# Four-layer attention backward on one core: chunk 0 of the window layers in 16 visits, layer 1's first visits inside the last linear tile

## The chip, the cores and the metric

The kernel runs on one core of a Trainium2 chip. The metric is the device time of one execution in microseconds (us): the median of repeated runs. A profile is one further execution, recorded instruction by instruction; its times are counted from the first instruction. Engines are named as in the profile: PE (TensorE; PEld are its weight loads), DVE (VectorE), ACT (ScalarE), POOL (GpSimd), SP (the queue that issues nearly every DMA).

## What is computed

A stack of four residual layers over x of shape [2048, 640] in bfloat16, and its gradient for a given `grad_out`: the output, the gradient of x, and those of four weight matrices.

```python
x = x + A(layernorm(x))   # layer 0: linear attention
x = x + B(layernorm(x))   # layer 1: sliding window
x = x + A(layernorm(x))   # layer 2
x = x + B(layernorm(x))   # layer 3
out, vjp = jax.vjp(f, x, wqkv_A, wo_A, wqkv_B, wo_B); grads = vjp(grad_out)
```

`A` has 32 heads of 20 columns with feature map `phi` and no softmax. `B` has the same heads, a causal softmax over a window of 256 rows.

## The kernel before, in words

Rows are handled in 16 tiles of 128 (`TT`), two tiles to a chunk (8 chunks). The stages follow each other: the forward of all layers (`forward`); the backward of layer 3's window attention (`core`); the linear backward of layer 2 (`plan_linear`, 16 tiles); `core` again for layer 1; then layer 0's linear backward together with the weight gradients.

**The order is written out by hand.** Each stage makes a list of (due slot, function), sorts it, and runs it slot by slot (`slots`, `plan`); the due slots are the lists in `PLACES`. Every engine executes its own instructions strictly in the order so recorded, SP's DMAs among them, so an instruction that waits holds all that stand behind it on its engine.

**A core** walks over visits (`core_visits`, `core_visit`). A visit has up to four blocks of 128 queries by 128 keys for two heads. In it PE makes the scores `s` (one PSUM buffer, pool `pS`), ACT makes `e = exp(s)`, POOL masks diagonal and far blocks (L803, L807). Three visits later PE makes `dp` (one PSUM buffer, `pD`) and DVE makes `ds = dp * e` (L792). Four visits later PE transposes `ds` (L814), and `st.lag` = 6 visits later it multiplies `ds` and `e` into `acc`. So the next `s` waits for the last `e`, and the next `dp` for the last `ds`. Chunk 0 has no earlier keys: six blocks where other chunks have twelve, in 24 visits of two blocks; chunks 1 to 7 have 24 visits each of up to four. In chunk 0 each visit also issues 8 transposes of the identity whose result is not used (`warm`, `thin` in `core`).

**Each chunk needs its gradients first** (`plan_before`): load `gb` and `ob` by DMA, transpose `gb` (`flip`), multiply by `WoT` (`prod`, L913 on DVE), sum over each head (`fold`, `split`: L921, L923, L930, L932, on POOL but for one tile of layer 1's chunk 0, which is on DVE) and transpose `ds` into `dT` (`flip8`, L941, copied by ACT at L942). For chunk c+1 this is spread over chunk c's visits; for chunk 0 it stands at the end of the stage before. The keys and queries of a quarter chunk come as slabs (`core_loads`), fetched one quarter ahead on SP.

**At the start of layer 3's core** the last slots of the forward (`tail`, up to seven) run as hooks of the first visits. The weights `WTB` (2.46 MB) come in one DMA at visit 15.

**At the start of layer 1's core** the last linear tile ends first: its products `dh` (PE, taken out of PSUM by ACT at L1184), `ln` (DVE L1193, L1195; the sum with the handed-over gradient on POOL at L1196), `ln2` (ACT L1203, POOL L1204) and the store `g<-lgn`. Then `core` begins. The slabs take over the memory of the linear stage's loads. The linear stage rotates over six PSUM buffers.

Of the kernel before, what the change touches and what calls it, by code (L numbers as in the profile page):

```python
# [15 lines left out]
P = 128  # L16
# [55 lines left out]
    sd=[0.7, 0, 0, 3, 3, 3, 3, 3.9, 0, 0, 3.2, 2.6, 3.3, 3.1],  # L72
    dj=[3, 21.9, 24, 3.5, 0.7, 8])


class Kern:
# [121 lines left out]

    def fetch(self, w, src):
        self.dma(w.rearrange("p a b -> p (a b)"), src)  # L200

# [82 lines left out]
    def forward(self, st):  # L284
# [108 lines left out]
        def begin_slabs():  # L393
            early.close()
            self.core_slabs(3, st.core)
            self.core_buffers(st, st.core)
        plan += [(END - 32, begin_core), (END - 6, begin_slabs)]
# [4 lines left out]
        def before(a):  # L402
            if a == 0:
                first_.update(enumerate(self.slots(self.plan_before(st, 3, 0, st.core, ((1, 2, 3, 4.5, 10), (2, 4, 5, 10, 12))), 16)))
            if first_[a] is not None:
                first_[a]()
# [301 lines left out]
    def core_visits(self, st, l, S, c, qr, dq):  # L708

        t0 = 2 * c  # L710
        w0 = max(t0 - 2, 0)
        for p in range(2):
            if c == 0:
                order = [[(0, 0), (1, 0), (1, 1)]] * 2
            else:
                order = [[(0, 0), (0, 1), (1, 1), (0, 2), (1, 2), (1, 3)], [(0, 0), (0, 1), (0, 2), (1, 2), (1, 3), (1, 1)]]
            units = [(gi, bi, kk) for gi in range(2) for bi, kk in order[gi]]
            m = len(units) // 3
            for v in range(3):
# [11 lines left out]
                u.first, u.last = v == 0, v == 2  # L731
                u.n = 24 * c + 6 * qr + 3 * p + v
                u.by_dma = self.by_dma(u.n)
                yield u
# [7 lines left out]
    def order(n):  # L742

        return ("FPA", "PFA", "PAF", "FAP", "AFP", "APF")[PLACES["fo"][n % 24] if 48 <= n < 192 else 0]

    WARM = (8, 5)
    TAIL = 5
# [11 lines left out]
    def core_visit(self, st, l, u, piece, on_act, thin):  # L759
# [63 lines left out]
        self.tick(0.5)  # L823
        for k in self.order(len(h) - 1):
            if parts[k] is not None:
                parts[k]()
# [61 lines left out]

    def plan_before(self, st, l, c, B, at=None, l0=0, quick=False):

# [10 lines left out]
        for i, (f0, p0, p1, sp, f8) in enumerate(at):  # L901
# [14 lines left out]
            def fold(i=i, t=t):  # L916
                R = B.ring[t % 4]
                assert x["n", i] == 2
                pr = x["pr", i] = B.sf.tile([P, H, DH], F32, name="prod")
                eng = nc.vector if quick and i == 0 else nc.gpsimd  # L920
                eng.tensor_tensor(out=pr, in0=R["ds"][:, :, 0:DH], in1=self.heads(x["o"][:, i, :]), op=ALU.mult)  # L921
# [3 lines left out]
            def split(i=i, t=t):  # L925
                R = B.ring[t % 4]
                m = DH // 4
                ds, pr = R["ds"], x["pr", i][:, :, 0:m]
                eng = nc.vector if quick and i == 0 else nc.gpsimd
                eng.tensor_scalar(out=ds[:, :, DH:DH + m], in0=pr, scalar1=-1.0, scalar2=None, op0=ALU.mult)  # L930
# [163 lines left out]
    def plan_linear(self, st, lp, l, t, X, WT, g_out):  # L1094

        nc = self.nc
        sv = self.sv[l]
        i = t % 2
# [88 lines left out]
        def ln():  # L1187
# [7 lines left out]
            nc.vector.tensor_scalar(out=x["s1"], in0=ac[:, 0:1], scalar1=ac[:, 1:2], scalar2=-1.0 / D, op0=ALU.add, op1=ALU.mult)  # L1195
            nc.gpsimd.tensor_tensor(out=x["dh"], in0=x["dh"], in1=L["g"][:, i, :], op=ALU.add)  # L1196

        def ln2():
            L = X[t // 2]
            if i == 0:  # L1200
                L["gn"] = lp.lo.tile([P, 2, D], BF, name="lgn")
            assert "s1" in x
            nc.scalar.activation(x["a"], L["hn"][:, i, :], ACT.Identity, bias=x["s1"], scale=x["s2"])  # L1203
            nc.gpsimd.tensor_tensor(out=L["gn"][:, i, :], in0=x["dh"], in1=x["a"], op=ALU.add)  # L1204
            if i == 1:
                self.put(13, self.pair(g_out, t // 2), L["gn"])
# [122 lines left out]

    def core_slabs(self, l, B):  # L1330
# [4 lines left out]
    def core_buffers(self, st, B):  # L1335
        st.lag = 6
        st.pe = self.pool(B.es, "pe", st.lag + 1, side=B.side)
        st.pd = self.pool(B.es, "pd", st.lag - 2, side=B.side)
        st.pt = self.pool(B.es, "pt", st.lag - 2, side=B.side)
# [42 lines left out]
    def core(self, st, l, g_out, B, hooks):  # L1382

        NC = TT // 2

        plan = []
        dq = {}
        for c in range(1, NC):
            plan += [(32 * (c - 1) + a, *f) for a, *f in self.plan_before(st, l, c, B)]
        for c in range(NC):  # L1390
# [6 lines left out]
        rest = [(max(a - off, 0), f) for a, f, *_ in plan if a * 0.75 >= nv]  # L1397
        rest = self.slots(rest, int(max(a for a, _ in rest)) + 1)

# [5 lines left out]
        on_act = [PLACES["xx"][n % 24] for n in range(nv)]  # L1405
        n = 0
        with ExitStack() as es:
            st.pS = self.pool(es, "pS", 1, bass.MemoryType.PSUM, "right")
            st.pD = self.pool(es, "pD", 1, bass.MemoryType.PSUM, "right")
            st.hist = []  # L1410
            for c in range(NC):
                for qr in range(4):
                    S = B.slabs.pop(0)
                    for i, u in enumerate(self.core_visits(st, l, S, c, qr, dq)):
                        for k, f in enumerate(hooks):
                            if int(k * 0.75) == n:
                                f()
# [4 lines left out]
                        if n == st.lag:  # L1422
                            st.pA = self.psum(es, "pA", 1)
                            dqp = self.pool(B.dqs, "dqp", 3, side="right")
                        if n % 24 == st.lag:
                            dq[c] = dqp.tile([P, 2, QT], BF, name="dq")
                        self.core_visit(st, l, u, slots[n], on_act[n], thin[n])
                        n += 1
            for _ in range(st.lag):
                self.core_visit(st, l, None, slots[n], on_act[n], thin[n])  # L1430
                n += 1
        return rest

# [12 lines left out]
    def passes(self):  # L1446
# [6 lines left out]
        with ExitStack() as rest:  # L1453
# [5 lines left out]
            def switch():  # L1459
                keep.close()  # L1460
                self.rest_pools(st, es)
            assert n3 <= 7
            hooks = tail[:-1] + [lambda: (tail[-1](), switch())] + [lambda: None] * (7 - n3)

            hooks += [lambda: None] * (70 - len(hooks))
            hooks[20] = lambda: self.fetch(st.WTB, self.WT["B"])
            hooks[40] = lambda: self.fetch(st.WoTA, self.WoT["A"])
            left3 = self.core(st, 3, self.gs[2], st.core, hooks)
            for f in left3[:8]:
# [7 lines left out]

            psl, le, lw, w1 = ExitStack(), ExitStack(), ExitStack(), ExitStack()
            WTA = self.pool(lw, "wa", 1).tile([P, NF, D], BF, name="WTA")
            st.ps = self.psum(psl, "pl", 6)  # L1480
            lp, B = self.linear_pools(lw, "left", 0), S()
# [14 lines left out]
            for t in range(TT):  # L1496
                plan += [(max(base + 8 * t + a, 0), f) for a, f in self.plan_linear(st, lp, 2, t, X, WTA, self.gs[1])]

            def begin():
                self.flush()  # L1500
                le.close()
                self.core_slabs(1, B)
            b0 = base + 8 * (TT - 1) + PLACES["n1"][0]
            plan.append((b0, begin))
            fs = self.plan_before(st, 1, 0, B, (PLACES["n1"][1:6], PLACES["n1"][6:11]), -10, True)
            plan += [(b0 + a, f) for a, f, *_ in fs if a < 20]
            hooks = self.slots([(a - 20, f) for a, f, *_ in fs if a >= 20], 8)
            for f in self.slots(plan, int(max(a for a, _ in plan)) + 1):
# [4 lines left out]
            lw.close()  # L1513
            psl.close()
            st.ps = st.ps2
            yield

            self.core_buffers(st, B)
            left1 = self.core(st, 1, self.gs[0], B, [f or (lambda: None) for f in hooks])
            for f in left1[:8]:  # L1520
# [136 lines left out]
```

## Time and profile before

| | |
|---|---|
| three runs | 2153.57, 2156.81 (median), 2165.6 us |
| the profiled execution, first to last instruction | 2161.7 us |
| PE busy | 2022.5 us (94%) |
| DVE, ACT, POOL busy | 1396.7, 1313.6, 1034.4 us |
| the forward of all layers | 0 to 665 us |
| layer 3's core, visits of chunk 0 | 665 to 708 us |
| layer 2's linear stage, full pace | 1138 to 1228 us |
| the last linear tile and layer 1's chunk 0 | 1228 to 1281 us |

The profiled execution is 4.9 us longer than the median of the runs. The view of stretches of the span gives, for each stretch, the time that each engine was busy and "PEclk", the clock that TensorE was granted as a share of full speed; it takes only the values 1 and 0.5, so an average between them tells what part of the stretch ran at half speed. The view in order of time gives, for a group of equal instructions, start, duration, engine, line, operation, what is written and read, and in brackets how long the engine had been idle before it and what ended that.

### The profile page before, as it was taken

How to read it: one execution, taken by the hardware profiler on the slowest of the kernel's cores; microseconds unless marked ns; L12 is line 12 of the kernel's file. 1: busy time of each engine (PE TensorE's matmuls, PEld its weight loads, DVE VectorE, ACT ScalarE, POOL GpSimd, SP SyncE). 2: the span in 40 equal slices, each digit the busy share in tenths (PEclk: the TensorE clock that was granted, in tenths of full speed). 3: DMA queues.
4: the chain of work that ended last, by engine and by line, in shares of the span. 5: the costliest groups of instructions: out<-in, count | busy, mean ns of one | idle time of the engine just before them, and what ended most of it. 6: DMA issues, size and time to landing. Idle time of an engine off the chain costs nothing.

```text
span 2161.7 us, 77035 instructions
## 1 busy us (share of the span) xinstructions
PE 2022.5 (94%) x32885; PEld 1566.0 (72%) x32885; DVE 1396.7 (65%) x2828; ACT 1313.6 (61%) x1866; POOL 1034.4 (48%) x1643
## 2 busy tenths in 40 slices
PE   8989998899988999999989999999998989999999
PEld 6667776677766877777768778777776888888644
DVE  7788886788854888888748769888886233320000
ACT  6558887478875787777637667777775133330000
POOL 1046666156666577777524466777765211220000
PEclk9999999999998999999989989999999999999999
DMA  7597876699984379988889824899888899989650
GB/s 253 195 230 205 215 203 174 199 228 213 221 204 135 94 160 189 189 191 180 185 269 265 213 82 102 191 191 191 177 181 204 272 296 250 267 203 276 194 164 21
DMA packets 658937, 425.46 MB, mean 197 GB/s; under 512 B 399264, under 2 KB 629408, under 8 KB 658208
## 3 DMA queue, kind: packets, MB, share of 16 engines
q1 hardware_dynamic: 658592, 420.52, 76.7%
q8 instruction: 257, 4.21, 0.8%
q14 instruction: 88, 0.72, 0.1%
HBM read 195.17 MB, written 144.70 MB: 157 GB/s over the span
## 4 chain that ended last, share of the span: by engine, by line
PE 51%; DVE 8%; DMA 7%; ACT 6%; issue 4%; POOL 3%; SPq 2%; DVEq 0%; ACTq 0%; POOLq 0%
PE dense L187 17%; PE wg L187 14%; DVE ds L792 5%; PE acc L187 4%; PE dp L187 3%; PE flip L207 3%; PE flip L814 2%; DMA pqb<-pqk 2%; SPq L131 2%; ACT e L788 2%; PE flip L218 1%; PE sT L187 1%; PE ops L187 1%; ACT eT L450 1%; ACT dsT L819 1%
## 5 line engine op out<-in xcount | busy, mean ns | idle before, releaser
L792 DVE TENSOR_TENSOR ds<-dp,e 128x1024 bf16<-128x1024 f32 (+1 forms) x384 | 444.0, 1156 | 122.0 <-PE s L187 76.7
L788 ACT ACTIVATE e<-s 128x1024 bf16<-128x1024 f32 (+1 forms) x384 | 375.0, 976 | 113.5 <-PE s L187 94.9
L450 ACT ACTIVATE eT<-sT 128x2048 bf16<-128x2048 f32 x180 | 338.3, 1880 | 94.9 <-PE sT L187 77.9
L187 PE MATMUL wg<-rhs,lhs 128*128 128x240 bf16 (+3 forms) x2880 | 372.2, 286 | 4.4 <-DMA lhs<-o 4.4
L187 PEld LDWEIGHTS <-lhs 128*128 128x128 bf16 x2880 | 261.4, 98 | 92.3 <-DMA lhs<-o 5.4
L807 POOL TENSOR_SCALAR_AFFINE_SELECT e<-e 128x256 bf16<-128x256 bf16 x512 | 207.5, 420 | 166.7 <-ACT e L788 163.4
L187 PEld LDWEIGHTS <-dqT 128*128 128x128 bf16 x1920 | 174.0, 98 | 61.5 <-issue 4.4
L458 POOL TENSOR_SCALAR_AFFINE_SELECT eT<-eT 128x512 bf16<-128x512 bf16 x256 | 163.8, 644 | 107.1 <-ACT eT L450 103.2
L187 PE MATMUL acc<-slabqs,ds 128*128 128x20 bf16 x2880 | 195.9, 172 | 2.6 <-ACT dq L876 0.3
L187 PE MATMUL acc<-ds,e 128*128 128x20 bf16 x2880 | 193.6, 171 | 0.0
L187 PEld LDWEIGHTS <-ds 128*128 128x128 bf16 x2880 | 173.3, 96 | 19.7 <-issue 15.3
L187 PE MATMUL dp<-slabT,dT 32*128 32x128 bf16 (+1 forms) x1952 | 150.0, 244 | 28.5 <-DVE ds L792 22.6
L803 POOL TENSOR_SCALAR_AFFINE_SELECT e<-e 128x512 bf16<-128x512 bf16 x224 | 143.3, 640 | 60.0 <-ACT e L788 57.8
L187 PEld LDWEIGHTS <-e 128*128 128x128 bf16 x2880 | 164.3, 96 | 5.8 <-issue 1.5
L1304 DVE CAST wr<-wg 128x240 bf16<-128x240 f32 (+3 forms) x54 | 24.5, 453 | 221.7 <-PE wg L187 215.6
L187 PE MATMUL dense<-WB,hnT 128*128 128x320 bf16 x960 | 161.8, 303 | 1.2 <-ACT hnT L210 0.7
L1196 POOL TENSOR_TENSOR dh<-dh,lg 128x640 f32<-128x640 f32 x32 | 46.0, 1438 | 241.7 <-DVE s L1193 219.1
L187 PE MATMUL dense<-WTA,dqT 128*128 128x320 bf16 x960 | 156.3, 299 | 2.5 <-DMA dqT<-dqa 2.2
L1302 ACT CAST wr<-wg 128x240 bf16<-128x240 f32 (+3 forms) x36 | 14.3, 397 | 236.8 <-PE wg L187 234.2
L814 PE MATMUL flip<-ident,ds 128*128 128x128 bf16 x1920 | 153.4, 221 | 3.4 <-DVE ds L913 3.4
L187 PE MATMUL dense<-WTB,dqT 128*128 128x320 bf16 x960 | 154.6, 302 | 0.0
L187 PE MATMUL s<-slabT,slabqT 32*128 32x128 bf16 (+1 forms) x1952 | 147.5, 246 | 4.5 <-ACT e L788 4.5
(184 smaller groups left out, 4473.0 us busy)
## 6 DMA issues: line engine op xcount, KB each, us to landing
T<-T SPq DMA_DIRECT2D x96, 256.0 KB, 3.7
s<-s SPq DMA_DIRECT2D x32, 512.0 KB, 3.2
slabT<-T SPq DMA_DIRECT2D x64, 256.0 KB, 3.6
dqkv<-dq SPq DMA_DIRECT2D x16, 960.0 KB, 6.6
dqkv<-dqa SPq DMA_DIRECT2D x32, 480.0 KB, 4.7
rhs<-dqkv SPq DMA_DIRECT2D x32, 480.0 KB, 5.9
rhs<-dqkv SPq DMA_DIRECT2D x16, 960.0 KB, 6.6
hn<-hn SPq DMA_DIRECT2D x64, 160.0 KB, 3.3
```

The source lines that it names most:

```text
L131: return self.nc.sync.dma_start(out=out, in_=in_, transpose=transpose)
L187: return self.nc.tensor.matmul(out, lhsT=lhsT, rhs=rhs, start=start, stop=stop, skip_group_check=True, **kw)
L207: self.nc.tensor.transpose(t[0:w, j, :], src[:, c0:c0 + w], self.ident)
L450: nc.scalar.activation(e, s, ACT.Exp)
L458: nc.gpsimd.affine_select(out=e, in_=e, compare_op=ALU.is_ge, fill=0.0, base=0, pattern=[[0, 4], [1, P]], channel_multiplier=-1)
L788: nc.scalar.activation(u.e[:, :, 0:w], s[:, :, 0:w], ACT.Exp)
L792: nc.vector.tensor_tensor(out=d.ds[:, :, 0:w], in0=d.dp[:, :, 0:w], in1=d.e[:, :, 0:w], op=ALU.mult)
L803: nc.gpsimd.affine_select(out=v, in_=v, pattern=[[0, 4], [1 if far else -1, P]], **kw)
L807: nc.gpsimd.affine_select(out=v, in_=v, pattern=[[0, 2], [1 if far else -1, P]], **kw)
L814: nc.tensor.transpose(ps[:, 4 * j + i, :], f.ds[:, j, i * P:(i + 1) * P], self.ident)
L1196: nc.gpsimd.tensor_tensor(out=x["dh"], in0=x["dh"], in1=L["g"][:, i, :], op=ALU.add)
L1304: nc.vector.tensor_copy(o[:, 0:w], ps[:, 0:w])
```

## The change

- Chunk 0 of both cores goes in 16 visits of three blocks. Visits are numbered from 8 (`V0`), so chunk 1 still begins at 24. What is due in chunk 0 is squeezed into the 16.
- `WTB` comes in five DMAs of 0.49 MB, 11 to 31 visits after the start; `WoTA` comes 36 after.
- Chunk 1's `gb` and `ob` are loaded ahead: in layer 3 with the first slabs (6 slots before the forward ends), in layer 1 twelve slots before the slabs (`BEF1`).
- `fold` and `split` for both tiles of chunk 0 are on DVE (`quick` = 2), in both layers.
- Layer 1's chunk 0 gradients begin 26 slots before the slabs (`BEF`), among linear tiles 12 to 15.
- Layer 1's first three visits are recorded in the last linear tile (`core` is now a generator, `next(c1)` at slots 4, 5, 6 after the slabs). For this the linear stage gives up two of its six PSUM buffers in that tile, and `pd`, `pt` and `pD` are only taken from the fourth visit on.
- In the last linear tile the two sums of the hand-over (`ln`, `ln2`) are on DVE, and the last pair's result lies in another pool (`st.sp`).

```diff
+TAILV = (0, 0, 1, 2, 3, 4, 5)
+B1_ = (4, 5, 6)
+BEF, BEF1 = -26, 14
...
         def begin_slabs():
             early.close()
-            self.core_slabs(3, st.core)
-            self.core_buffers(st, st.core)
+            self.core_slabs(st, 3, st.core)
+            st.core.next = self.plan_before(st, 3, 1, st.core)
+            st.core.next.pop(0)[1]()
...
-            m = len(units) // 3
-            for v in range(3):
+            nv = 3 if c else 2
+            m = len(units) // nv
+            for v in range(nv):
...
-                eng = nc.vector if quick and i == 0 else nc.gpsimd
+                eng = nc.vector if i < quick else nc.gpsimd
...
+        eng = nc.vector if l == 2 and t == TT - 1 else nc.gpsimd
...
-            nc.gpsimd.tensor_tensor(out=x["dh"], in0=x["dh"], in1=L["g"][:, i, :], op=ALU.add)
+            eng.tensor_tensor(out=x["dh"], in0=x["dh"], in1=L["g"][:, i, :], op=ALU.add)
...
-            nc.gpsimd.tensor_tensor(out=L["gn"][:, i, :], in0=x["dh"], in1=x["a"], op=ALU.add)
+            eng.tensor_tensor(out=L["gn"][:, i, :], in0=x["dh"], in1=x["a"], op=ALU.add)
...
+                if c == 1:
+                    a = self.V0 / 0.75 + a * (1 - self.V0 / 24) if a < 32 else a
...
-        n = 0
+        n = self.V0
...
+                        if n == self.V0 + 3:
+                            self.core_buffers(st, B)
+                            st.pD = self.pool(es, "pD", 1, bass.MemoryType.PSUM, "right")
...
+            for k in range(5):
+                hooks.setdefault(11 + 5 * k, []).append(lambda k=k: self.fetch(st.WTB, self.WT["B"], 3 * k, 3 * k + 3))
+            hooks.setdefault(36, []).append(lambda: self.fetch(st.WoTA, self.WoT["A"]))
...
-            st.ps = self.psum(psl, "pl", 6)
+            four = self.psum(ps4, "pl", 4)
+            st.ps = Turns((four, four, self.psum(psl, "pm", 2)))
...
+            def narrow():
+                st.ps = four
...
-            fs = self.plan_before(st, 1, 0, B, (PLACES["n1"][1:6], PLACES["n1"][6:11]), -10, True)
-            plan += [(b0 + a, f) for a, f, *_ in fs if a < 20]
+            c1 = self.core(st, 1, self.gs[0], B, {})
+            plan += [(b0, begin), (b0 - 1, narrow), (b0 + B1_[0] - 0.01, psl.close)]
+            plan += [(b0 + a, lambda: next(c1)) for a in B1_]
+            fs = self.plan_before(st, 1, 0, B, (PLACES["n1"][1:6], PLACES["n1"][6:11]), 0, 2)
+            plan += [(b0 + BEF + a, f) for a, f, *_ in fs] + [(b0 + BEF + BEF1, chunk1)]
```

More of the change, by code (lines that the diff above doesn't have):

```diff
@@ L73, with __init__, tile @@
     dj=[3, 21.9, 24, 3.5, 0.7, 8])
+TAILV = (0, 0, 1, 2, 3, 4, 5)
+B1_ = (4, 5, 6)
+BEF, BEF1 = -26, 14
+class Turns:
+    def __init__(self, pools):
+        self.pools, self.n = pools, 0
+    def tile(self, *a, **k):
+        self.n += 1
+        return self.pools[self.n % len(self.pools)].tile(*a, **k)
 class Kern:
@@ L197, in banked, with fetch @@
                 self.after(i, first)
-    def fetch(self, w, src):
-        self.dma(w.rearrange("p a b -> p (a b)"), src)
+    def fetch(self, w, src, a=0, b=None):
+        b = w.shape[1] if b is None else b
+        self.dma(w[:, a:b].rearrange("p a b -> p (a b)"), src[:, a * D:b * D])
     def flip(self, ps, sb, src, name, w, n, step, eng, cols=None, **kw):
@@ L403, in before @@
             if a == 0:
-                first_.update(enumerate(self.slots(self.plan_before(st, 3, 0, st.core, ((1, 2, 3, 4.5, 10), (2, 4, 5, 10, 12))), 16)))
+                first_.update(enumerate(self.slots(self.plan_before(st, 3, 0, st.core, ((1, 2, 3, 4.5, 10), (2, 4, 5, 10, 12)), 0, 2), 16)))
             if first_[a] is not None:
@@ L730, in core_visits @@
                         u.runs.append([gi, bi, kk, j, 1])
-                u.first, u.last = v == 0, v == 2
-                u.n = 24 * c + 6 * qr + 3 * p + v
+                u.first, u.last = v == 0, v == nv - 1
+                u.n = 24 * c + 6 * qr + 3 * p + v if c else self.V0 + 4 * qr + 2 * p + v
                 u.by_dma = self.by_dma(u.n)
@@ L744, in order @@
         return ("FPA", "PFA", "PAF", "FAP", "AFP", "APF")[PLACES["fo"][n % 24] if 48 <= n < 192 else 0]
+    V0 = 8
     WARM = (8, 5)
@@ L823, in core_visit @@
         self.tick(0.5)
-        for k in self.order(len(h) - 1):
+        for k in self.order(self.V0 + len(h) - 1):
             if parts[k] is not None:
@@ L887, in slots, with plan_before @@
         return [(lambda fs=fs: [f() for f in fs]) if fs else None for fs in out]
-    def plan_before(self, st, l, c, B, at=None, l0=0, quick=False):
+    def plan_before(self, st, l, c, B, at=None, l0=0, quick=0):
         at = at or (PLACES["bf"][:5], PLACES["bf"][5:])
@@ L928, in split @@
                 ds, pr = R["ds"], x["pr", i][:, :, 0:m]
-                eng = nc.vector if quick and i == 0 else nc.gpsimd
+                eng = nc.vector if i < quick else nc.gpsimd
                 eng.tensor_scalar(out=ds[:, :, DH:DH + m], in0=pr, scalar1=-1.0, scalar2=None, op0=ALU.mult)
@@ L1200, in ln2 @@
             if i == 0:
-                L["gn"] = lp.lo.tile([P, 2, D], BF, name="lgn")
+                L["gn"] = (st.sp.tile([P, 2, D], BF, name="gn", bufs=2) if l == 2 and t == TT - 2
+                           else lp.lo.tile([P, 2, D], BF, name="lgn"))
             assert "s1" in x
             nc.scalar.activation(x["a"], L["hn"][:, i, :], ACT.Identity, bias=x["s1"], scale=x["s2"])
-            nc.gpsimd.tensor_tensor(out=L["gn"][:, i, :], in0=x["dh"], in1=x["a"], op=ALU.add)
+            eng.tensor_tensor(out=L["gn"][:, i, :], in0=x["dh"], in1=x["a"], op=ALU.add)
             if i == 1:
@@ L1328, in core_pads, with core_slabs @@
             self.nc.gpsimd.memset(R["ds"][:, :, DH + DH // 2:HP], 0.0)
-    def core_slabs(self, l, B):
+    def core_slabs(self, st, l, B):
         B.slab = self.pool(B.es, "slab", 2, side=B.side)
@@ L1333, in core_slabs, with core_buffers @@
         B.slabs = [self.core_loads(l, 0, 0, B)]
-    def core_buffers(self, st, B):
         st.lag = 6
         st.pe = self.pool(B.es, "pe", st.lag + 1, side=B.side)
+    def core_buffers(self, st, B):
         st.pd = self.pool(B.es, "pd", st.lag - 2, side=B.side)
@@ L1384, in core @@
         NC = TT // 2
+        st.lag = 6
         plan = []
@@ L1388, in core @@
         for c in range(1, NC):
-            plan += [(32 * (c - 1) + a, *f) for a, *f in self.plan_before(st, l, c, B)]
+            for a, *f in B.next if c == 1 else self.plan_before(st, l, c, B):
+                if c == 1:
+                    a = self.V0 / 0.75 + a * (1 - self.V0 / 24) if a < 32 else a
+                plan.append((32 * (c - 1) + a, *f))
         for c in range(NC):
@@ L1397, in core @@
         rest = [(max(a - off, 0), f) for a, f, *_ in plan if a * 0.75 >= nv]
-        rest = self.slots(rest, int(max(a for a, _ in rest)) + 1)
+        B.rest = self.slots(rest, int(max(a for a, _ in rest)) + 1)
         thin = [PLACES["th"][n % 24] for n in range(nv)]
@@ L1405, in core @@
         on_act = [PLACES["xx"][n % 24] for n in range(nv)]
-        n = 0
+        n = self.V0
         with ExitStack() as es:
             st.pS = self.pool(es, "pS", 1, bass.MemoryType.PSUM, "right")
-            st.pD = self.pool(es, "pD", 1, bass.MemoryType.PSUM, "right")
             st.hist = []
@@ L1414, in core @@
                     for i, u in enumerate(self.core_visits(st, l, S, c, qr, dq)):
-                        for k, f in enumerate(hooks):
-                            if int(k * 0.75) == n:
-                                f()
+                        for f in hooks.get(n - self.V0, ()):
+                            f()
+                        if n == self.V0 + 3:
+                            self.core_buffers(st, B)
+                            st.pD = self.pool(es, "pD", 1, bass.MemoryType.PSUM, "right")
                         if i == 0:
@@ L1421, in core @@
                             B.slabs.append(self.core_loads(l, *divmod(4 * c + qr + 1, 4), B))
-                        if n == st.lag:
+                        if n == self.V0 + st.lag:
                             st.pA = self.psum(es, "pA", 1)
                             dqp = self.pool(B.dqs, "dqp", 3, side="right")
-                        if n % 24 == st.lag:
+                        if n == (24 * c or self.V0) + st.lag:
                             dq[c] = dqp.tile([P, 2, QT], BF, name="dq")
@@ L1428, in core @@
                         n += 1
+                        yield
             for _ in range(st.lag):
@@ L1431, in core @@
                 n += 1
-        return rest
     def rest_pools(self, st, es):
@@ L1461, in switch @@
                 self.rest_pools(st, es)
[L1462 to L1468, printed above, removed]
+            hooks = {}
+            for k, f in enumerate(tail):
+                hooks.setdefault(TAILV[k], []).append(f)
+            assert TAILV[n3 - 1] < 6
+            hooks[TAILV[n3 - 1]].append(switch)
+            for k in range(5):
+                hooks.setdefault(11 + 5 * k, []).append(lambda k=k: self.fetch(st.WTB, self.WT["B"], 3 * k, 3 * k + 3))
+            hooks.setdefault(36, []).append(lambda: self.fetch(st.WoTA, self.WoT["A"]))
+            for _ in self.core(st, 3, self.gs[2], st.core, hooks):
+                pass
+            left3 = st.core.rest
             for f in left3[:8]:
@@ L1476, in passes @@
             yield
-            psl, le, lw, w1 = ExitStack(), ExitStack(), ExitStack(), ExitStack()
+            psl, ps4, le, lw, w1 = ExitStack(), ExitStack(), ExitStack(), ExitStack(), ExitStack()
             WTA = self.pool(lw, "wa", 1).tile([P, NF, D], BF, name="WTA")
-            st.ps = self.psum(psl, "pl", 6)
+            four = self.psum(ps4, "pl", 4)
+            st.ps = Turns((four, four, self.psum(psl, "pm", 2)))
             lp, B = self.linear_pools(lw, "left", 0), S()
@@ L1497, in passes, with chunk1 @@
                 plan += [(max(base + 8 * t + a, 0), f) for a, f in self.plan_linear(st, lp, 2, t, X, WTA, self.gs[1])]
+            def chunk1():
+                B.next = self.plan_before(st, 1, 1, B)
+                B.next.pop(0)[1]()
             def begin():
@@ L1501, in begin @@
                 le.close()
-                self.core_slabs(1, B)
+                self.core_slabs(st, 1, B)
+            def narrow():
+                st.ps = four
             b0 = base + 8 * (TT - 1) + PLACES["n1"][0]
-            plan.append((b0, begin))
-            fs = self.plan_before(st, 1, 0, B, (PLACES["n1"][1:6], PLACES["n1"][6:11]), -10, True)
-            plan += [(b0 + a, f) for a, f, *_ in fs if a < 20]
-            hooks = self.slots([(a - 20, f) for a, f, *_ in fs if a >= 20], 8)
+            c1 = self.core(st, 1, self.gs[0], B, {})
[3 more added lines that the diff above has]
+            plan += [(b0 + BEF + a, f) for a, f, *_ in fs] + [(b0 + BEF + BEF1, chunk1)]
             for f in self.slots(plan, int(max(a for a, _ in plan)) + 1):
@@ L1513, in passes @@
             lw.close()
-            psl.close()
+            ps4.close()
             st.ps = st.ps2
             yield
-            self.core_buffers(st, B)
-            left1 = self.core(st, 1, self.gs[0], B, [f or (lambda: None) for f in hooks])
+            for _ in c1:
+                pass
+            left1 = B.rest
             for f in left1[:8]:
```

## The prediction, made before the changed kernel ran

> **What bounds the kernel now.** I read first the shares of the engines, then the clock by slices, then the stretches at the places that the change touches, and last the instructions in order of time there.
>
> ```profile
> PE 2022.5 (94%) x32885; PEld 1566.0 (72%) x32885; DVE 1396.7 (65%) x2828; ACT 1313.6 (61%) x1866; POOL 1034.4 (48%) x1643
> PEclk9999999999998999999989989999999999999999
> ```
>
> PE is busy for 94% of the span: time can only be won where PE is idle, runs at half clock, or does work that is not needed. The clock is 8 tenths in three slices of 54 us: the 13th and the 24th hold the starts of the two cores, where I look closer; the 21st is the end of layer 3's core, which the change leaves alone.
>
> ```profile
> 657.00:660.40 3.40, 2.06 (x50) 1.47 (x47) 1.24 (x3) 1.74 (x2) 3.32 (x7) 1.00 0.16 53
> 660.40:663.90 3.50, 2.50 (x41) 2.31 (x42) 0.00 (x0) 1.90 (x2) 3.50 (x7) 0.51 0.00 0
> 663.90:667.30 3.40, 2.65 (x38) 1.77 (x38) 0.75 (x2) 1.58 (x3) 1.46 (x3) 0.50 0.05 17
> 667.30:670.70 3.40, 0.00 (x0) 0.00 (x0) 0.00 (x0) 0.99 (x2) 0.77 (x2) 0.50 0.86 249
> 670.70:674.10 3.40, 2.93 (x18) 1.86 (x19) 0.49 (x1) 1.29 (x2) 0.41 (x1) 0.50 0.46 168
> 674.10:677.50 3.40, 3.15 (x19) 1.35 (x17) 1.58 (x3) 0.60 (x1) 0.41 (x1) 0.50 0.16 51
> ...
> 1237.30:1240.70 3.40, 1.58 (x19) 1.13 (x18) 1.27 (x4) 1.25 (x3) 2.85 (x3) 1.00 0.14 11
> 1240.70:1244.10 3.40, 1.62 (x14) 1.03 (x14) 0.00 (x0) 2.81 (x5) 3.15 (x5) 0.50 0.88 268
> 1244.10:1247.50 3.40, 2.52 (x21) 1.31 (x18) 0.00 (x0) 2.28 (x4) 3.24 (x6) 0.50 0.32 111
> 1247.50:1251.00 3.50, 2.56 (x28) 1.82 (x28) 2.28 (x5) 0.73 (x2) 0.77 (x2) 0.50 0.00 0
> 1251.00:1254.40 3.40, 3.40 (x32) 2.43 (x30) 1.50 (x3) 0.72 (x2) 0.68 (x2) 0.50 0.56 154
> ```
>
> The columns are stretch, its length, busy time of PE, PEld, DVE, ACT and POOL, clock, DMA share, GB/s. At layer 3's start PE is idle for 1.34 + 1.00 + 0.75 + 3.40 + 0.47 + 0.25 = 7.2 us and half of its 11.2 us at clock 0.5 is lost: 5.6. At layer 1's start it is idle for 5.4 us, and half of 10.1 us is lost: 5.05. That makes 23.3 us to be had at most from the starts. What causes them, in order of time:
>
> ```profile
> 654.34 1.35 POOL L921 TENSOR_TENSOR prod<-ds,ob 128x640 f32<-128x640 bf16 x1
> 655.76 1.41 POOL L923 TENSOR_TENSOR prod<-prod 128x320 f32<-128x320 f32 x2
> ...
> 664.32 0.64 POOL L458 TENSOR_SCALAR_AFFINE_SELECT eT<-eT 128x512 bf16<-128x512 bf16 x1
> ```
> ```profile
> 670.91 0.71 PE L207 MATMUL flip<-ident,gb 128*128 128x128 bf16 x5 [3.85 <-DMA gb<-in_grad_out_dram]
> ```
> ```profile
> 1242.44 0.40 PE L187 MATMUL s<-slabT,slabqT 32*128 32x128 bf16 x4 [3.56 <-ACT e L788]
> ```
> ```profile
> 1247.92 0.69 DVE L792 TENSOR_TENSOR ds<-dp,e 128x512 bf16<-128x512 f32 x1 [7.94 <-DMA g<-lgn]
> ```
>
> The forward's last masks run on POOL without a gap up to 664.96, behind the folds of chunk 0; PE then waits 3.85 us for a load; at layer 1's start `e` stands on ACT behind the whole chain of the last hand-over; `ds` waits for a store.
>
> **Sum of the change, part by part.** All on the profiled execution of 2161.7 us.
>
> *Sixteen visits.* The products for the blocks stay. PE loses 8 x 8 = 64 unused transposes per layer; eight take 0.45 us of weight loads at full clock (1258.28, `ident` x8), so 0.056 us each and 3.6 us per layer. PE is busy for 9.79 of 10 us from 685 to 695, so this lies on the path. On ACT 24 exponentials of 0.60 become 16 of about 0.81 (between 0.60 for 512 columns and 1.02 for 1024), on DVE 24 `ds` of 0.69 become 16 of about 0.95, on POOL 32 masks of 0.41 become 16 of 0.64: all less, beside PE. The cycle of the single `dp` buffer (0.35 + 0.95 + 0.2) stays under a visit of about 1.8 us on PE. With visits of three blocks, six visits of lag hold back more work into chunk 1; it is only shifted.
>
> *Weights in five parts, WoTA later.* The one DMA at visit 15 holds the slab behind it (`slabks`, issued at 692.12, landed at 703.46, where 2.3 us are usual), yet PE shows no wait there: slabs come a quarter ahead. Value 0; from 0 to a gain of 2, since a quarter of four visits (7.2 us) would feel the 11.3 us. Four more issues of about 0.45 us on SP delay nothing.
>
> *Layer 3's start.* Two folds of 1.35 + 1.41 + 0.68 + 0.57 = 4.0 us leave POOL; on DVE one costs 1.02 + 0.86 + 0.26 + 0.33 = 2.5 (1234.37 to 1237.2), and DVE is busy for 1.3 of 10 us from 655 to 665. The last `eT` then starts at 658.8, 2.46 after that at 656.34, ends at 660.7, three masks follow, and the first `s` runs at 662.8, not 665.4. The load of `gb` has long landed. ACT's row now decides: `e` 0.8, `gT` 0.7, `dT` 1.0, `e` 0.8, so the third `s` comes at 666.6, `dp` at 668.4 and the fifth visit at 671, if the clock holds; at half clock throughout I get 674.4. Twelve blocks stand at that point; before, they did at 680.8 (the seventh visit). I take 673: a gain of 7.8. The other 48 transposes give 2.7. **Together 10.5 us.**
>
> *Layer 1's start.* Zero point is the ten transposes of the last tile's `dqa`, 1229.33 before. From there the seventh visit (1253.98) was 24.65 away, of which 5.5 of PE work is chunk 0's preparation, which now stands ahead (two flips 0.44, four products 0.84, two `flip8` 0.61). So 19.2 is to be beaten. Now: `slabqT` is issued at about 0.9 (it waits for those transposes) and needs 3.4 to land (1230.21 to 1233.65), so the first `s` is at 4.4, with PE idle for 1.8; `s` again at 6.0 and 7.9, each after an `e`; the last linear product ends at 9.7. **The added wait:** on DVE the two sums now stand ahead of the first `ds`. ACT takes `dh` out (10.5), DVE runs L1193 and L1195 (1.1) and the sum (taken at 0.9, between 0.62 for L1143 and 1.02 for L921, both 128x640), ACT `lna` (0.92) only after the fourth `e`, then the second sum, then `ds` 0.95. The `dp` of the fifth visit waits for that: 14.4, with PE idle for about 2.5. On POOL the two sums cost 1.40 + 1.54; there the masks would be late instead. One us I add for DVE in the linear stage, where it is busy for 77.59 of 90 us and takes 6.9 more in two and a half tiles (between 0 and 3), with four PSUM buffers for one tile inside that; two for half clock after these idle times (0 to 5). 19.2 - 17.4 = 1.8, and 2.7 for 48 transposes. **Together 4.5 us.** The store that `ds` waited for is gone by the other pool; what is late next is the second sum.
>
> Total 15.0: 2161.7 - 15.0 = 2146.7 for such an execution. The median of the runs lies 4.9 lower, so I predict 2156.8 - 15.0 = 2141.8, rounded to **2142**.
>
> **The clock, and the Trainium skill.** The row from 1237.30 shows the clock falling with PE busy for 1.58 of 3.40 us, that from 657.00 with 2.06 of 3.40. The Trainium skill, "TensorE: Matmul & The Clock Gate", section "Why this matters for your kernels", wants no idle gap above some 3 us: one window of idle brings half clock. These rows disagree: a window that is half busy was enough. By that rule the new gaps (1.8 and 2.5 us) would leave the clock at full speed, and the sum would be that of the first rival below.
>
> **Rivals.**
> 1. *The clock holds at both starts.* Then layer 3's fifth visit is at 671 (9.8 + 2.7) and layer 1's at 15.4 (3.8 + 2.7): 19 us, 2138. For it: no single gap is as long as 3.56. Against: the two rows above. Chance 0.15.
> 2. *The new wait on DVE takes what the early visits give.* Half clock for four windows, as now: layer 3 gains 6.4 + 2.7, layer 1 loses 1.8 against 2.7 (its fifth visit 6 us later than 15): 10 us, 2147; with 3 us lost on DVE in the linear tiles, 2150. For it: the chain of `dh`, sum, `lna`, sum, `ds` is worked out from rows and longer than any cover. Chance 0.27.
> 3. *Fewer unused transposes, and the clock falls inside chunk 0.* Eight per 1.3 us become eight per 1.8. About 28 us of PE work per layer at half clock every other window costs 14 each: 2157 - 15 + 28 = 2170, slower. It decides where idle and small products together leave a 3.4 us window like that from 657.00. Against: from 745 to 755, in chunk 1 with about five per visit, PE is busy for 9.84 of 10 at clock 1.00. Chance 0.08.
> 4. *It doesn't do what it says:* the visits in the linear tile wait for slabs and preparation crowds DVE, so that layer 1 loses 5 and layer 3 gains half: about 2157. Chance 0.10.
>
> The forecast itself has 0.40: 2137 to 2146.
>
> **Range and chances.** The bounds of the single terms (2 for the weights, 3 for DVE, 5 for the clock, 3.4 at layer 3) spread the forecast and its neighbours from 2131, which is 26 us and so most of the 23.3 + 7.2 that there is, to 2147; rivals 2 and 4 reach 2156. So 2131 to 2156. About 0.5% (10.8 us) is what a measurement of this kernel can tell from no change: faster than 2146 has the forecast, rival 1 and some of rival 2, 0.62; within, the rest of 2 and rival 4, 0.30; slower, 0.08.
>
> **What would show it.** PE: 32885 instructions less about 193 (129 transposes, 64 products made into fewer). Layer 3: the `gb` wait of 3.85 is gone, POOL's last mask before its core ends near 662.6, first `s` near 663. Layer 1: first `s` about 4.4 us after the last `dqa` transposes, and a wait of some 2.5 us of the fifth `dp` on DVE `ds`. Chunk 0's 16 visits near 1.8 us. Wrong: half clock inside chunk 0; linear tiles 12 to 15 longer than 6.6 us plus their 5.5 of preparation; slabs that land late behind the parts of the weights.

## The result and the profile after

The changed kernel takes 2146.28 us (median of 8 runs, 2139.59 to 2152.29), the kernel before 2162.15 in the same session: ratio 0.9927, 95% interval 0.9912 to 0.9943, so 15.8 us shorter (12.3 to 19.0). Forecast: 15.0. The time itself was forecast as 2142; it is 4 us longer because the kernel before takes 2162.15 in these eight runs and took 2156.8 in the three that the forecast started from. The profiled execution has a span of 2145.0 us, 16.7 less than before. The head of its page, which answers to the two lines shown of before:

```profile
PE 2009.7 (94%) x32692; PEld 1555.7 (73%) x32692; DVE 1398.7 (65%) x2817; ACT 1310.1 (61%) x1846; POOL 1014.0 (47%) x1594
...
PEclk9999999999999999999989999999999999999999
```

PE has 193 instructions less, the number forecast, and is busy for 12.8 us less. The 13th and the 24th slice are back at 9. The starts by stretches (columns as in the prediction):

```profile
662.70:666.10 3.40, 2.57 (x24) 1.57 (x22) 0.75 (x2) 2.81 (x5) 1.20 (x2) 0.50 0.51 143
666.10:669.50 3.40, 3.40 (x20) 1.56 (x19) 1.15 (x3) 0.95 (x2) 0.71 (x2) 0.50 0.31 103
1242.95:1246.35 3.40, 3.40 (x31) 2.22 (x29) 2.29 (x4) 1.16 (x2) 2.76 (x4) 0.50 0.01 5
```

These are all the stretches at half clock near the starts: 6.8 us at layer 3 where there were 17.1, 3.4 us at layer 1 where there were 13.7. What leads up to them, by the instructions in order of time:

```profile
660.55 0.41 PE L203 MATMUL ops<-s,eT 128*128 128x21 bf16 x10 [1.02 <-POOL eT L476]
...
662.06 0.34 PE L203 MATMUL s<-slabT,slabqT 32*128 32x128 bf16 x4
662.33 0.45 PE L224 MATMUL flip<-ident,gb 128*128 128x128 bf16 x5
...
671.07 0.23 PE L203 MATMUL dp<-slabT,dT 32*128 32x128 bf16 x2
...
1232.52 0.34 PE L203 MATMUL s<-slabT,slabqT 32*128 32x128 bf16 x4 [1.18 <-DMA slabqT<-T]
...
1239.06 1.12 DVE L1217 TENSOR_TENSOR dh<-dh,lg 128x640 f32<-128x640 f32 x1
1239.24 0.92 ACT L1225 ACTIVATE lna<-lhn,s,s 128x640 f32<-128x640 bf16 x1 [0.49 <-DVE s L1216]
1240.28 0.82 DVE L1226 TENSOR_TENSOR gn<-dh,lna 128x640 bf16<-128x640 f32 x1
1241.02 0.95 DVE L812 TENSOR_TENSOR ds<-dp,e 128x768 bf16<-128x768 f32 x1
1242.03 0.23 PE L203 MATMUL dp<-slabT,dT 32*128 32x128 bf16 x2 [3.30 <-DVE ds L812]
```

Layer 3: the flip of `gb` follows the first `s` with no wait (3.85 us before). Layer 1: the added wait is there, 3.30 us where 2.5 was forecast, behind sum, `lna` and sum as worked out. The first `s` comes 3.7 us after the first of the last `dqa` transposes (4.4 forecast), and chunk 0's visits take 2.05 and 2.1 us on average, the starts included, where about 1.8 was forecast.

**How the experiments are compared.** Single half-clock windows in stages that nobody touched move a whole run by several us. So the trace is cut at instructions that every kernel has. Stretch A runs from one fixed `eT` of ScalarE in the forward's last 40 us to the first `e` of chunk 2 of layer 3; stretch B from the last `dqa` transpose of layer 2's tile 11 to the first `e` of chunk 2 of layer 1. In brackets the time at half clock inside (one window is 3.4). The median is of runs, the ratio is against before with its interval.

| kernel | median | ratio | A | B |
|---|---|---|---|---|
| before | 2162.15 | 1 | 131.3 (17.1) | 126.0 (13.7) |
| changed | 2146.28 | 0.9927 (0.9912 to 0.9943) | 122.0 (6.8) | 119.4 (3.4) |
| 24 visits | 2156.16 | 0.9983 (0.9968 to 0.9999) | 126.0 (6.8) | 125.2 (6.8) |
| 160 unused transposes | 2156.60 | 0.9972 (0.9953 to 0.9991) | 125.5 (10.2) | 123.8 (3.4) |
| 48 unused, sums on GpSimd | 2144.33 | 0.9925 (0.9897 to 0.9952) | 121.6 (10.2) | 120.4 (13.7) |
| none unused | 2147.58 | 0.9945 (0.9923 to 0.9967) | 121.4 (20.5) | 119.4 (10.2) |
| folds on GpSimd | 2148.46 | 0.9942 (0.9919 to 0.9965) | 127.2 (20.5) | 120.0 (6.8) |
| `gb` late | 2153.72 | 0.9972 (0.9950 to 0.9994) | 131.4 (20.5) | 120.1 (3.4) |
| weights in one | 2147.44 | 0.9940 (0.9916 to 0.9964) | 123.2 (10.2) | 119.6 (3.4) |
| no early visits | 2143.80 | 0.9918 (0.9890 to 0.9947) | 121.2 (6.8) | 118.2 (3.4) |
| layer norm later | 2150.51 | 0.9937 (0.9916 to 0.9958) | 121.8 (6.8) | 118.0 (0) |
| sums on GpSimd | 2144.84 | 0.9927 (0.9904 to 0.9950) | 121.4 (6.8) | 116.8 (0) |
| no early, sums on GpSimd | 2142.17 | 0.9921 (0.9894 to 0.9949) | 124.1 (10.2) | 116.0 (0) |
| no early, preparation late | 2143.88 | 0.9920 (0.9892 to 0.9948) | 121.3 (6.8) | 117.2 (6.8) |

The change gains 9.3 us in A and 6.6 in B, together 15.9: that is the whole gain of the runs. Kernels with the same code in a stretch and as much half clock differ there by under 1 us (A: 121.2 to 122.0; B: 119.4 to 120.1), which is what a reading of A or B can tell.

### The profile page after: what moved, and what is told of

Same layout as the page of the kernel before. It is cut to its first block, busy times and chain, and to the rows that moved or that the text cites. A ratio compares the mean times of both kernels' runs of the same rounds, so it can differ in the third digit from the quotient of the medians.

```text
span 2145.0 us, 76508 instructions
## 1 busy us (share of the span) xinstructions
PE 2009.7 (94%) x32692; PEld 1555.7 (73%) x32692; DVE 1398.7 (65%) x2817; ACT 1310.1 (61%) x1846; POOL 1014.0 (47%) x1594
## 4 chain that ended last, share of the span: by engine, by line
PE 52%; DVE 7%; ACT 6%; DMA 6%; issue 4%; POOL 3%; SPq 2%; DVEq 0%; ACTq 0%; POOLq 0%
PE dense L203 18%; PE wg L203 15%; DVE ds L812 5%; PE acc L203 4%; PE dp L203 3%; DMA pqb<-pqk 3%; PE flip L224 2%; PE flip L834 2%; ACT e L808 2%; SPq L147 2%; PE sT L203 1%; ACT eT L468 1%; PE ops L203 1%; ACT dsT L839 1%; PE flip L235 1%
## 5 line engine op out<-in xcount | busy, mean ns | idle before, releaser
L827 POOL TENSOR_SCALAR_AFFINE_SELECT e<-e 128x256 bf16<-128x256 bf16 x448 | 182.6, 422 | 138.3 <-ACT e L808 137.0
L476 POOL TENSOR_SCALAR_AFFINE_SELECT eT<-eT 128x512 bf16<-128x512 bf16 x256 | 164.2, 645 | 112.9 <-ACT eT L468 108.9
L823 POOL TENSOR_SCALAR_AFFINE_SELECT e<-e 128x512 bf16<-128x512 bf16 x256 | 162.8, 636 | 85.5 <-ACT e L808 83.0
L479 POOL TENSOR_SCALAR_AFFINE_SELECT eT<-eT 128x512 bf16<-128x512 bf16 x224 | 143.9, 642 | 14.9 <-ACT eT L468 13.5
```

The costliest lines, as they stand in the source:

```text
L476: nc.gpsimd.affine_select(out=e, in_=e, compare_op=ALU.is_ge, fill=0.0, base=0, pattern=[[0, 4], [1, P]], channel_multiplier=-1)
L479: nc.gpsimd.affine_select(out=e, in_=e, compare_op=ALU.is_ge, fill=0.0, base=-1, pattern=[[0, 4], [-1, P]], channel_multiplier=1)
L823: nc.gpsimd.affine_select(out=v, in_=v, pattern=[[0, 4], [1 if far else -1, P]], **kw)
L827: nc.gpsimd.affine_select(out=v, in_=v, pattern=[[0, 2], [1 if far else -1, P]], **kw)
```

## The experiments

All are made from the changed kernel.

**1. Fewer visits, or fewer unused transposes?** Chunk 0 in 24 visits; and 16 visits with as many unused transposes as 24 had.

```diff
-            nv = 3 if c else 2
+            nv = 3
...
-                u.n = 24 * c + 6 * qr + 3 * p + v if c else self.V0 + 4 * qr + 2 * p + v
+                u.n = 24 * c + 6 * qr + 3 * p + v
...
-    V0 = 8
+    V0 = 0
```


> Chunk 0 of both layers in 24 visits of two blocks again, all else as changed. My theory (the saving is the unused transposes, eight per visit): 3.6 us per layer come back, 64 more transposes each, the run is about 7 us longer than the changed kernel (2153), and both starts up to the fifth visit stay where they are, less about 2 us per layer because a point of twelve blocks is then the seventh visit. Rival A (every visit has a fixed price of its own): 16 visits at half a microsecond each come on top, 15 us longer. Rival B (the transposes are needed to hold the clock): no loss, or shorter.

```diff
+    for n in range(12, 24):
+        thin[n] = 13 + (n % 3 == 0)
```


> 16 visits, but the twelve transposes of ds in chunk 0 are each preceded by 13 or 14 unused ones, 160 per layer as with 24 visits, where the changed kernel has 96. My theory: 64 x 0.056 = 3.6 us per layer, 7 us longer than the changed kernel. Rival A (fixed price of a visit): clearly less than the kernel with 24 visits loses. Rival B (they hold the clock or stand beside a wait): under 2 us.

The transposes alone cost 3.5 us in A and 4.4 in B; 0.7 of the 3.5 is a half-clock window ahead of the first `s`, in untouched work. That leaves 7.2 of 7.9, as forecast. The 24 visits cost 4.0 and 5.8, and of the last 1.7 is one more half-clock window. So the visits themselves have no price that A and B can show: rival A has fallen, and so has B, at this size.

**2. How few transposes will do?** None in chunk 0; and four to a visit (4 in place of 0 in the diff), with the sums on GpSimd as in experiment 5.

```diff
+    for n in range(12, 24):
+        thin[n] = 0
```


> None of the 96 unused transposes of chunk 0 (both layers), all else as changed. My theory (at 0.056 us each they only take PE's time once the starts are over): 5.4 us shorter per layer, 11 in all (2136). Rival B (they keep the clock up): half-clock windows appear inside chunk 0 beyond those of the starts, each costing 1.7 us, and the gain is under 4 us or a loss. A third way: PE waits for ds or e instead, and part of the 5.4 us turns into idle time at full clock.

> Four unused transposes ahead of each of chunk 0's twelve, not eight (48 fewer per layer), with the sums on GpSimd. If the clock holds: 2.7 us per layer shorter than the kernel with the sums alone moved (chunk 1 of layer 3 starts 29.8 us after the first e, not 32.5). If four are too few: half-clock windows inside chunk 0 as without any, 1.7 us each, and no gain.

My theory for none fell. 192 transposes less, by the rows 10.8 us, and the stretches are 0.6 us and nothing shorter. The clock took it back: 20.5 us more at half clock (13.7 in A, 6.8 in B) lose 10.2. Nor is it one profile alone: the granted clock of the ten whole runs without unused transposes averages 0.979, that of the ten runs with the weights in one transfer, in the same session, 0.984. Stretches of the kernel without them, in chunk 0 of layer 3:

```profile
685.40:688.80 3.40, 3.25 (x53) 2.50 (x52) 2.40 (x4) 2.29 (x5) 1.27 (x2) 0.53 0.69 242
688.80:692.20 3.40, 3.40 (x64) 2.63 (x61) 2.15 (x4) 2.75 (x6) 1.27 (x2) 0.50 0.06 18
692.20:695.60 3.40, 3.40 (x64) 2.98 (x64) 1.75 (x3) 2.61 (x4) 1.11 (x2) 0.50 0.98 300
```

and of the changed kernel at the same place:

```profile
685.40:688.80 3.40, 2.28 (x59) 1.93 (x56) 1.68 (x3) 1.71 (x5) 0.83 (x2) 1.00 0.50 182
688.80:692.20 3.40, 3.40 (x79) 2.98 (x76) 2.58 (x4) 2.77 (x5) 1.30 (x3) 1.00 0.15 40
692.20:695.60 3.40, 3.40 (x88) 3.06 (x86) 1.64 (x3) 3.17 (x6) 1.05 (x2) 1.00 0.93 274
```

PE is busy for all of 3.40 us in both, at clock 0.50 without the unused transposes and at 1.00 with them, and even the stretch with 2.28 us busy is at full clock. (These stretches are not cut where the clock changes. Cut there, the least busy window of chunk 0 in the changed kernel, 686.59 to 690.01, has 2.76 us and the clock holds; the one ahead of the fall in the other kernel, 682.21 to 685.62, has 2.69, its waits 0.3 us at most.) Half clock lasts 13.7 us here and 6.8 in chunk 0 of layer 1. With four to a visit it lasts 3.4, as chunk 1 of layer 3 begins, and 13.7 in chunk 0 of layer 1, so B is 3.6 us longer than with the sums alone moved. There it follows a window in which PE waited 1.9 us for a `ds` (1.0 with eight); whether the missing transposes or that longer wait let the clock fall isn't separated. With eight or more, layer 3 has one window (folds on GpSimd; weights in one, just behind chunk 0) or two (`gb` late) behind its start in three kernels, and none in the others: eight is just about enough. This is rival 3 of the prediction. The Trainium skill, "TensorE: Matmul & The Clock Gate", section "Part 4: PE-mode transpose", says that a transpose doesn't count as a busy PE in the same way; here the clock falls when the unused ones, which the trace lists as MATMUL by `ident`, are taken out.

**3. Layer 3's start: the folds and the early load.**

```diff
-    first_.update(enumerate(self.slots(self.plan_before(st, 3, 0, st.core, ((1, 2, 3, 4.5, 10), (2, 4, 5, 10, 12)), 0, 2), 16)))
+    first_.update(enumerate(self.slots(self.plan_before(st, 3, 0, st.core, ((1, 2, 3, 4.5, 10), (2, 4, 5, 10, 12)), 0, 0), 16)))
...
-    fs = self.plan_before(st, 1, 0, B, (PLACES["n1"][1:6], PLACES["n1"][6:11]), 0, 2)
+    fs = self.plan_before(st, 1, 0, B, (PLACES["n1"][1:6], PLACES["n1"][6:11]), 0, 1)
```


> The folds and splits of chunk 0 where they were: layer 3's four steps on GpSimd, in layer 1 the first tile's on VectorE and the second's on GpSimd. My theory (the two folds of 4.0 us hold back the forward's last masks, and the idle time starts a long half clock): layer 3's first e comes 3 to 4 us later (662.4 in the changed kernel), half clock lasts four windows or more there instead of two, chunk 1 of layer 3 starts 6 to 8 us later. Rival E (chunk 0 of layer 3 goes by the row of exponentials on ScalarE and has slack): only the 3 to 4 us of the first e, or less, and two windows. Layer 1: within 1 us by both.

```diff
     st.core.next = self.plan_before(st, 3, 1, st.core)
-    st.core.next.pop(0)[1]()
```


> Layer 3's load of chunk 1's gradients at its old place in the plan instead of ahead. My theory: the transposes of gb wait for it again, 3 to 4 us of PE in chunk 0, and chunk 2 of layer 3 starts 2 to 5 us later after the forward's end. Rival I (the wait was the long half clock's doing, chunk 0 has other work by then): under 1 us, no wait for gb.

With the folds on GpSimd the first `s` comes 2.0 us later after the fixed `eT` and half clock lasts four windows at the start, not two; A is 5.2 us longer. About 1.0 of that is a half-clock window of the forward: behind it every `eT`, the last too, comes 1.1 us later than in the kernel before, which has the same folds. So the folds alone cost the first `s` 1.0 us and A 4.2. My theory holds in kind, with less than the 6 to 8 us expected; this rests on one profile, since the interval of the whole runs holds the changed kernel's ratio. The late load costs more than expected, 9.4 us, the whole gain of A:

```profile
668.69 0.72 PE L224 MATMUL flip<-ident,gb 128*128 128x128 bf16 x5 [5.20 <-DMA gb<-in_grad_out_dram]
```

PE waits for 5.20 us, longer than the 3.85 of before, since the first `s` is now earlier and the flip stands in the first visit; half clock then lasts 13.7 us, and 6.8 more at 694.6. The two losses add up to more than the gain of A: each of the two waits alone is enough to bring the long half clock.

**4. The weights in parts.**

```diff
-    for k in range(5):
-        hooks.setdefault(11 + 5 * k, []).append(... 3 * k, 3 * k + 3))
-    hooks.setdefault(36, []).append(... WoTA ...)
+    hooks.setdefault(10, []).append(lambda: self.fetch(st.WTB, self.WT["B"]))
+    hooks.setdefault(22, []).append(... WoTA ...)
```


> The weights in one transfer at the eleventh visit, and WoTA at the twenty-third, as before. My theory: no PE wait on a slab above 1 us appears in layer 3's chunks 0 and 1, the time from the first e to chunk 2 is that of the changed kernel within 1 us. Rival G (four visits to a quarter are too short for a slab behind that transfer): a wait for slabqT or slabks of 2 to 4 us in chunk 0's last quarters.

The one transfer takes 9.2 us to land, the parts 4.0 to 5.5. A is 1.2 us longer with one more window (1.7 us); the longest PE wait for a slab is 0.8 us, in the changed kernel it is 1.1. No effect is seen.

**5. Layer 1's start: early visits, sums, preparation.**

```diff
-    plan += [(b0 + a, lambda: next(c1)) for a in B1_]
```


> The first three visits of layer 1 after the last linear tile instead of in it; sums on VectorE and preparation stay as changed. My theory: the idle times of PE in the tile are no longer filled, fifth visit 2 to 5 us later after the last ten transposes of dqa than the 13.3 of the changed kernel, and so much longer in all. Rival C (the wait of dp on the ds behind the sums took the gain of the early visits): that wait of 3.3 us goes, and the time is the same within 1 us.

My theory fell: without the early visits B is 1.2 us shorter. The fifth visit's `dp` runs 12.0 us after the last `dqa` transpose, in the changed kernel 12.8, because its 3.30 us wait is gone: the sums are over (1229.93) before `ds` has its `dp`. Rival C.

```diff
-    eng = nc.vector if l == 2 and t == TT - 1 else nc.gpsimd
+    eng = nc.gpsimd
```


> The two hand-over sums of layer 2's last tile on GpSimd again (1.40 and 1.54 us there, 1.12 and 0.82 on VectorE), all else as changed. My theory: GpSimd's masks come late instead, the first ds still waits for nothing behind the sums, and the time from the last ten dqa transposes to chunk 1 of layer 1 changes by less than 1.5 us either way. Rival F (the sums on VectorE are what makes the early visits worthless): that time is 2 to 3 us shorter, as with the layer norm recorded later (35.6 against 37.0).

Rival F: 34.4 us to chunk 1, not 37.0, B 2.6 shorter, of which the one half-clock window that is gone can be up to 1.7. The fifth `dp` waits 1.33 us, no longer 3.30:

```profile
1232.23 0.95 DVE L812 TENSOR_TENSOR ds<-dp,e 128x768 bf16<-128x768 f32 x1
1232.28 1.40 POOL L1217 TENSOR_TENSOR dh<-dh,lg 128x640 f32<-128x640 f32 x1 [1.62 <-DVE s L1214]
1232.41 0.92 ACT L1225 ACTIVATE lna<-lhn,s,s 128x640 f32<-128x640 bf16 x1 [0.50 <-DVE s L1216]
1233.24 0.23 PE L203 MATMUL dp<-slabT,dT 32*128 32x128 bf16 x2 [1.33 <-DVE ds L812]
```

`ds` runs beside the sum on GpSimd, not behind it.

In the next kernel the tile's layer norm leaves the plan and is recorded after the fourth and the fifth visit (its pool stays open for so long):

```diff
-    lw.close()
+    for f in lns:               # ln, ln2 of the last tile
+        next(c1)
+        f()
```


> The last tile's layer norm (VectorE sums and the lna of ScalarE) recorded behind the first ds and the second ds of layer 1, not ahead of them. My theory: the first ds starts with its dp, the wait of 3.3 us of the fifth dp goes, chunk 0 ends 2.5 to 3.5 us sooner. Rival D (something else is late next: e on ScalarE, the matrix clock still at half): the wait moves to an s that waits for e, and less than 1 us is gained.

Half right: the fifth `dp` is at 1234.83, 2.8 us sooner after the transposes, but the sixth now waits, behind the first sum. B is 1.4 us shorter, no more than the one window that is gone.

```profile
1236.23 1.82 DVE L1217 TENSOR_TENSOR dh<-dh,lg 128x640 f32<-128x640 f32 x1
1237.98 0.94 DVE L812 TENSOR_TENSOR ds<-dp,e 128x768 bf16<-128x768 f32 x1
1238.98 0.23 PE L203 MATMUL dp<-slabT,dT 32*128 32x128 bf16 x2 [2.03 <-DVE ds L812]
```

Two combinations: both undone together, and early visits undone with the preparation at its old places.

> No early visits and the hand-over sums on GpSimd: what is left of layer 1's start is the preparation ahead in the linear tiles and the fewer unused transposes. My theory: from the last ten dqa transposes to chunk 2 of layer 1 83 to 85 us (86.3 in the changed kernel, 84.9 without early visits, 83.8 with the sums on GpSimd), so the early visits and the sums on VectorE together cost 1.5 to 3 us and gain nothing. Rival C (the early visits pay once the sums no longer stand before ds): 85 or more, longer than with the sums alone moved.

```diff
-    plan += [(b0 + BEF + a, f) ...] + [(b0 + BEF + BEF1, chunk1)]
+    plan += [(b0 + (a or -10), f) ... if a < 20] + [(b0 + 19, chunk1)]
+    late[3] = [f for a, f, *_ in fs if a >= 20]
```


> No early visits, and the preparation of layer 1's chunk 0 at its old places, in the last linear tile and behind it, its last flip in the fourth visit; sums on VectorE. My theory (it is the preparation ahead that brings layer 1's gain): tiles 12 to 15 are shorter by 5.5 to 7 us, the time from the last ten dqa transposes to chunk 2 longer by 8 to 12 (93 to 97, against 84.9 without early visits), 2 to 5 us net loss. Rival H (preparation costs the same wherever it stands): net loss under 1 us.

The first came out as expected: 83 us to chunk 2, B 3.3 us shorter than in the changed kernel. So the early visits gain nothing with the sums on GpSimd either: B is 116.8 with them and 116.0 without, and the fifth `dp` runs 10.9 us after the last `dqa` transpose in both. In the second my theory fell: tiles 12 to 15 are 6.5 us shorter (26.3 against 32.8), the start 5.8 longer than without early visits, B 1.1 us shorter even with 3.4 us more half clock. Having the preparation ahead gains nothing: not the net loss of 2 to 5 us but, as rival H has it, none, and if anything the old places are cheaper. None of these kernels is shown to beat the changed one in whole runs: their intervals all hold its ratio.

## Why the prediction was right, and where it was not

- *Size.* Forecast 15.0, measured 15.8 by the runs and 15.9 by the two stretches. That the sum fits so well is partly luck: layer 3 gave 1.2 us less than its share, layer 1 2.1 more, and layer 1 by another cause than the one forecast.
- *Sixteen visits, 2 x 3.6 us.* 7.2, so right, and it is transposes, not visits.
- *Layer 3's start, 10.5 with its transposes.* 9.3. The clock, which I set between full and half throughout, fell for two windows. One step was mis-sized: the first `s` was to be 2.6 us earlier and is 1.0 earlier after the fixed `eT` (40.16 to 39.15), since GpSimd now waits for the forward's exponentials, 1.24 us ahead of its last mask but two. The fifth visit's `s` still comes 48.2 us after that `eT`, where the 673 of the forecast meant 47.8. The early load, which has one sentence there, decides as much as the folds.
- *Layer 1's start, 4.5.* 6.6, and the step behind it failed. I let the start win 1.8 us by the early visits. They win nothing: the wait that they bring (3.30 us) costs what they fill, as rival 2 has it. That is not the whole reason, since they win nothing with the sums on GpSimd either; what else holds them is not shown. But rival 2's half clock of four windows did not come (one did). What brings the gain in their place: about 4 us of transposes and three half-clock windows less, 5.1 us at most, part of which was idle time anyway. The transposes and two of the three windows are in the kernel without early visits and with the preparation late as well (B 117.2 against 126.0). That kernel still has 16 visits, the sums on VectorE and `gn` in the other pool; the 7.94 us wait of `ds` for a store is gone in it. That this store made the old half clock is argued only; it wasn't tried by itself.
- *Crowding in the linear tiles, 5.5 + 1.* 6.8 (26.1 to 32.8): right.
- *Weights, 0.* Right within what can be seen.
- *Rival 3,* the clock falling inside chunk 0, did not come in the changed kernel, with eight transposes to a visit, and did with four and with none: the clock does fall, and the change's number leaves little room.

## What to carry to other kernels

Price a moved step by undoing it alone in a stretch cut at instructions that all kernels share: here that tells 1 us, where the interval of whole runs is 7 to 12 us wide. Work moved into another stage's idle time need not win anything: here the early visits stood in line behind the sums on VectorE, and with the sums elsewhere the fifth `dp` came no sooner for them. At layer 3's start either of two waits was enough for the long half clock: removing one of them brought half of A's gain or nothing until the other was gone too.

## What the hardware showed that I had not expected

A PE that the profile shows as busy for 3.40 of 3.40 us can stay at clock 0.50 for four windows on end (685.62 to 699.27 in the kernel without unused transposes), behind a window with 2.69 us busy, while the changed kernel keeps 1.00 through and after one with 1.92 (1229.30 to 1232.71, in the last linear tile): the busy share doesn't tell what sets the clock, and the 128x128 transposes by `ident` seem to do more for it than the work that is left in chunk 0 without them. The Trainium skill, "TensorE: Matmul & The Clock Gate", section "Part 1: The HAM clock gate (the "warmup" mystery)", has the clock up after one busy window of 3.4 us; the length of the window agrees (each of the half-clock times above is a whole multiple of it), the busy window is not enough here. What is counted was not measured by itself. The sum of 128x640 on VectorE took 1.12 us in the changed kernel and 1.82 in the one with the layer norm later. In that kernel GpSimd ran its own products at the same time (L941 from 1235.47), and they too were longer, 1.91 us where 1.35 is seen in the changed kernel, so the two engines may have held each other up; that wasn't tried by itself.
